# Token mixing moved behind the attention, and a new order for the first head: an attention and MLP-mixer kernel on one core

## Chip, core and metric

One core of a Trainium2 chip. The metric is the device time of one execution in microseconds (us), the lower the better; it is given as the median of repeated runs.

## What is computed

```python
# attention: B=2, H=8, S=768, D=64, 16 centroids for each head
q_assign = argmax(q_n @ c_n.T)          # q, k, centroids normalized; k_assign alike
scores = where(q_assign[:, None] == k_assign[None, :], q @ k.T / 8, -1e9)
x = softmax(scores) @ v                 # then heads side by side: x is [2, 768, 512]
# first mixer
xt = x.transpose(0, 2, 1)
u = x + (relu(xt @ w_tok1) @ w_tok2).transpose(0, 2, 1)    # token mixing, 256 wide
x = u + relu(u @ w_ch1) @ w_ch2                            # channel mixing, 1536 wide
# second mixer
theta = x @ w_theta
u = x + w_tok_r @ (x * cos(theta)) + w_tok_i @ (x * sin(theta))
out = u + relu(u @ w_ch)
```

The weights come as 64-bit floats; the kernel converts them on the chip.

## The kernel before

**Numbers.** A float32 operand is split into a rounded high part and the rest (names that end in `h` and `l`), and a product is three matmuls: low by high, high by low, high by high (`mm3`). `split_sb` and `split_ps` make such a pair. `load_w` fetches a 512 KB block of 64-bit weights by the SP queue into one of three buffers (`wraw`), and converts it: two copies on ACT (L100, L101), a shift and a combination on DVE (L103, L104), an addition on POOL (L107), and then a split. The addition is the last reader of the raw buffer.

**Attention.** There are 48 units: 2 batches, 8 heads, 3 pairs of 128-row query tiles (`b, h, u`; the index `n` of the loop runs over them). Tile names carry batch, head, query tile: `nm175` belongs to batch 1, head 7, tile 5. For each unit `scores` makes 8 matmuls of 384 columns and for each of two query tiles a row maximum on DVE (`nm`, L359) and an exponential on ACT (`e`, L361); `turn`, one unit later, transposes `e` in three pieces of four transposes (L376) and splits each into `ph` and `pl`, either by ACT and DVE (kind "A") or by ACT and POOL (kind "C": a copy `pr`, then `ph` and `pl`, L386 and L387); `values`, two units later, makes 12 matmuls of 256 columns (L399), copied and added into `xt` (`tmp` on ACT, L404; `xt` on DVE, L406). `masks` finds the centroid of each query and key of a pair of heads (`sim`, four DVE steps, `pp`, `oh`); the result goes as extra rows 64 to 79 into the operands `q2` and `k2`. `natural` transposes a finished pair of heads into the residual `xn`.

**First pair.** `load_pair` loads heads 0 and 1 together (`ql00`, `kl00`: 128 rows). For the operands `qh`, `q2`, `k1`, `k2` of heads 0 and 1, `prep_first` loads each of them again, twice each, to have a head's 64 rows on both halves of the partitions. All of `masks(0, 0)`, the placing of the centroids and the second head's operands stand ahead of the first unit. Matmuls on a constant tile (`warm_up`, 17, 4, 20 and 18 of them) run on TensorE at the start.

**Token mixing.** The six blocks of w_tok1 and w_tok2 are loaded and converted in units 2, 6, 10, 14, 18 and 22 (`W_AT`), each behind the mask rows' transfers. `tokens(b, half)` mixes 256 of the 512 columns of one batch: 36 matmuls `g` and 36 `h` of 256 columns, so 288 in all four calls. From unit 18 on one step of it (a split, a `g` of 18 matmuls, an `h` of 6) is written behind each unit; calls that are left follow the last unit.

**Behind it.** `u_turn` transposes `xn` (48 transposes, `u`), and from there the channel mixing starts (`r`), followed by the second mixer.

**Order.** The order on each engine is fixed at build time by a list scheduler, so code is a priority rather than a place; `issue_after` holds code back behind an instruction. Each engine runs its own rows in order, so what waits holds up all that stands behind it on that engine.

Of the kernel before, what the change touches and what calls it, by code (L numbers as in the profile page):

```python
# [18 lines left out]
P = 128  # L19
# [26 lines left out]
WARM = (17, 4, 20, 18)  # L46
# [3 lines left out]
def tile_model(ctx: ExitStack, tc: tile.TileContext, qT, kT, v, cent, w1, w2, wc1, wc2, wth, wri, wch, out):  # L50
# [40 lines left out]
    def load_w(src, name, pool=None):  # L91
# [18 lines left out]
        split_sb(h, l, w, "pa"[wcount[0] % 2], "p")  # L110
# [12 lines left out]
    with ExitStack() as actx:  # L123
# [45 lines left out]
        for j in range(2):  # L169
            r, n = slice(64 * j, 64 * j + 64), slice(96 + CL * j, 96 + CL * j + CL)  # L170
            nc.vector.tensor_copy(out=cst[r, n], in_=cps[r, CL * j : CL * j + CL])
# [33 lines left out]
        for t in q2 + k2:  # L205
            nc.gpsimd.memset(t[64:128, :].bitcast(F32), 0.0)

        def masks(b, pr):
# [28 lines left out]
            turned = nc.vector.transpose(out=eqT, in_=eq)  # L237
            marks.setdefault("eqT", turned)
# [4 lines left out]
            nc.tensor.matmul(pp, ltri, eqT, start=True, stop=True)  # L243
            nc.vector.scalar_tensor_tensor(out=oh, in0=pp, scalar=0.0, in1=eqT, op0=ALU.is_equal, op1=ALU.mult)
            if first:
                for a in range(2):
                    n = slice(a * NH, a * NH + NH)
                    r = 32 * a
                    nc.vector.tensor_copy(out=q2[0][64 : 64 + CL, n], in_=oh[r : r + CL, :])
                    r = 64 + 32 * a  # L250
                    if a == 0:
                        nc.scalar.activation(  # L252
                            out=k2[0][64 : 64 + CL, n], in_=oh[r : r + CL, :], func=AF.Copy, scale=BIG, bias=-BIG
                        )
                    else:
                        nc.vector.tensor_scalar(
                            out=k2[0][64 : 64 + CL, n], in0=oh[r : r + CL, :], scalar1=BIG, scalar2=-BIG,
                            op0=ALU.mult, op1=ALU.add,
                        )
# [7 lines left out]
        def prep_first(b, h):  # L267
# [15 lines left out]
            return qh, q2[i], k1, k2[i], load_v(b, h)  # L283

# [59 lines left out]
        def scores(b, h, u, ops):  # L344
# [3 lines left out]
            for j in range(2):  # L348
# [3 lines left out]
                for half in range(2):  # L352
                    n = slice(half * NH, half * NH + NH)
                    nc.tensor.matmul(ps[:, half, :NH], qh[:, c], k1[:, n], start=True, stop=False)  # L354
                    last = nc.tensor.matmul(ps[:, half, :NH], ql[:, c], kk[:, n], start=False, stop=True)  # L355
                    if (b, h, u) == (0, 0, 0):
                        marks["scores"] = last
                nm = ap.tile([P, 1], F32, tag="nm", bufs=4, name=f"nm{b}{h}{qt}")
                nc.vector.tensor_reduce(out=nm, in_=ps[:, :, :NH], axis=AX.XY, op=ALU.max, negate=True)  # L359
                e = ap.tile([P, S], F32, tag="e", bufs=4, name=f"e{b}{h}{qt}")  # L360
                nc.scalar.activation(  # L361
# [6 lines left out]
        def turn(b, h, u, es):  # L368

            pr = []  # L370
            for j in range(NT // 2):
                ps = ps_t.tile([P, 2, 256], F32, tag="t", name=f"t{b}{h}{u}{j}")
                for i in range(2):
                    for a in range(2):
                        kt = 2 * j + a
                        nc.tensor.transpose(ps[:, a, i * P : i * P + P], es[i][:, kt * P : kt * P + P], ident)  # L376
# [33 lines left out]
        def tokens(b, half):  # L410

            cols = slice(half * 256, half * 256 + 256)
            xs, gs = [], []

            def split_x(s):
                h, l = (fp.tile([P, 256], F32R, tag="fx", bufs=12, name=f"x{k}{b}{half}{s}") for k in "hl")
                split_sb(h, l, xn[b * NT + s][:, cols], XS[0], XS[1])
                xs.append((h, l))

            def up(t):  # L420
                ps = ps_t.tile([P, 512], F32, tag="t", name=f"g{b}{half}{t}")[:, :256]
                lw = []
                for s in range(NT):
                    o = (s % 2) * 256 + t * P
                    lw.append(tuple(w[:, o : o + P] for w in w1s[s // 2]))
                mm3(ps, list(zip(lw, xs)), True, True)
                h, l = (fp.tile([P, 256], F32R, tag="fg", bufs=4, name=f"g{k}{b}{half}{t}") for k in "hl")
                nc.scalar.activation(out=h, in_=ps, func=AF.Relu)
                nc.vector.scalar_tensor_tensor(
                    out=l, in0=ps, scalar=0.0, in1=h.bitcast(F32), op0=ALU.max, op1=ALU.subtract  # L430
                )
                gs.append((h, l))

            def down(s):
                ps = ps_t.tile([P, 512], F32, tag="t", name=f"h{b}{half}{s}")[:, :256]
                lw = []
                for t in range(NTT):
                    o = t * 256 + (s % 2) * P
                    lw.append(tuple(w[:, o : o + P] for w in w2s[s // 2]))
                mm3(ps, list(zip(lw, gs)), True, True)  # L440
                x = xn[b * NT + s][:, cols]
                nc.vector.tensor_tensor(out=x, in0=ps, in1=x, op=ALU.add)

            for s in range(NT):
                split_x(s)
                yield
            for t in range(NTT):
                up(t)
                yield
            yield  # L450
            for s in range(NT):
# [325 lines left out]
```

## Time and profile before

| | us |
|---|---|
| median of 3 runs (lowest to highest) | 691.19 (689.98 to 693.18) |
| profiled execution, its own time | 691.88 |
| its span | 690.2 |
| TensorE, matmuls busy | 659.0 |
| VectorE (DVE) busy | 436.5 |
| ScalarE (ACT) busy | 372.8 |
| GpSimd (POOL) busy | 387.2 |
| first row maximum starts | 17.26 |
| first matmul of the channel mixing starts | 312.32 |

Times in the trace count from the start of the span; 1.7 us of the execution's time lie outside it. A matmul's busy time includes its way through the array, so matmuls overlap and "busy" is more than the pace.

### The profile page before, as it was taken

To read this page: it belongs to the slowest core of one execution; us is meant where nothing else is said; L and a number is where in the kernel's file an instruction comes from. 1 tells how busy PE (TensorE), PEld (TensorE's weight loads), DVE (VectorE), ACT (ScalarE), POOL (GpSimd) and SP (SyncE) were. 2 spreads that over 40 slices of the span, in tenths; PEclk is the share of its full clock that TensorE was granted. 3 is DMA by queue.
4 is the path that set the end of the run, shared out by engine and by line. 5 is a ranking of instruction groups with operands and counts; after the bars stand their busy time and mean duration, and the time that the engine had idled before them with its cause. 6 is when DMAs were issued, how large, how long until landed. Compare 5 with 4: busy or idle time off the path is not lost.

```text
span 690.2 us, 10585 instructions
## 1 busy us (share of the span) xinstructions
PE 659.0 (95%) x3772; PEld 578.1 (84%) x3772; DVE 436.5 (63%) x710; ACT 372.8 (54%) x722; POOL 387.2 (56%) x376
## 2 busy tenths in 40 slices
PE   7899989889999999999999999999999999999998
PEld 4798878788998999897888888888888777888886
DVE  6788788978888968558664533445657876523122
ACT  3687768676968777526553431135668684320000
POOL 8977779685866664437884640331456797432000
PEclk9899989999999999999999999999999999999999
DMA  9545645476344330003442321030021233320001
GB/s 264 142 108 165 173 106 146 104 222 180 81 93 92 86 76 1 1 1 123 134 142 92 122 91 33 9 114 2 0 62 61 88 95 93 123 61 32 16 30 47
DMA packets 24533, 62.27 MB, mean 90 GB/s; under 512 B 4320, under 2 KB 7584, under 8 KB 24480
## 3 DMA queue, kind: packets, MB, share of 16 engines
q1 hardware_dynamic: 24480, 61.59, 32.1%
q8 instruction: 30, 0.49, 0.3%
q14 instruction: 23, 0.19, 0.1%
HBM read 40.44 MB, written 3.15 MB: 63 GB/s over the span
## 4 chain that ended last, share of the span: by engine, by line
PE 74%; DVE 6%; DMA 6%; ACT 5%; POOL 4%; issue 3%; SPq 2%; ACTq 0%; POOLq 0%; DVEq 0%
PE o L399 7%; PE t L376 6%; PE r L118 5%; PE r L119 5%; PE r L120 5%; PE c L118 5%; PE c L119 5%; PE c L120 5%; PE y L120 4%; PE y L118 4%; PE y L119 4%; PE s L354 3%; PE s L355 3%; DMA w_raw<-w 3%; ACT e L361 2%
## 5 line engine op out<-in xcount | busy, mean ns | idle before, releaser
L359 DVE TENSOR_REDUCE nm<-s 128x1 f32<-128x768 f32 x96 | 90.9, 949 | 20.9 <-PE s L355 20.3
L361 ACT ACTIVATE e<-s,nm 128x768 f32<-128x768 f32 x96 | 86.9, 906 | 23.0 <-DVE nm L359 12.7
L376 PE MATMUL t<-ident,e 128*128 128x128 f32 x576 | 80.6, 275 | 5.9 <-DVE pl L86 4.7
L399 PE MATMUL o<-ph,vs 128*128 128x256 f32 x288 | 77.3, 298 | 3.0 <-DVE xt L406 3.0
L354 PE MATMUL s<-k,qh 128*128 128x384 f32 x192 | 70.7, 369 | 9.0 <-ACT e L361 6.8
L376 PEld LDWEIGHTS t<-ident,e 128*128 128x128 f32 x576 | 67.8, 142 | 10.5 <-DVE pl L86 4.3
L399 PE MATMUL o<-pl,vs 128*128 128x256 f32 x288 | 74.8, 291 | 0.3 <-POOL pl L387 0.3
L86 DVE TENSOR_TENSOR pl<-t,ph 128x512 fp32r<-128x512 f32 x96 | 62.9, 678 | 6.5 <-ACT ph L85 4.8
L355 PE MATMUL s<-k,q 128*128 128x384 f32 x192 | 65.7, 343 | 1.3 <-ACT k L252 1.3
L85 ACT ACTIVATE ph<-t 128x512 fp32r<-128x512 f32 x96 | 54.9, 598 | 17.6 <-PE t L376 14.8
L387 POOL TENSOR_TENSOR pl<-pr,ph 128x512 fp32r<-128x512 f32 x48 | 62.9, 1310 | 2.0
L386 POOL TENSOR_SCALAR ph<-pr 128x512 fp32r<-128x512 f32 x48 | 30.3, 632 | 57.6 <-ACT pr L382 51.4
L399 PEld LDWEIGHTS o<-ph,vs 128*128 128x128 f32 x288 | 56.1, 195 | 4.0 <-DVE xt L406 3.7
L118 PE MATMUL r<-ul,c_h 128*128 128x512 f32 x144 | 56.7, 394 | 0.0
L399 PEld LDWEIGHTS o<-pl,vs 128*128 128x128 f32 x288 | 56.1, 195 | 0.5 <-POOL pl L387 0.5
L118 PE MATMUL y<-zl,k_h 128*128 128x512 f32 x144 | 56.1, 390 | 0.0
L120 PE MATMUL y<-zh,k_h 128*128 128x512 f32 x144 | 56.1, 389 | 0.0
L119 PE MATMUL y<-zh,k_l 128*128 128x512 f32 x144 | 56.0, 389 | 0.0
L119 PE MATMUL r<-uh,c_l 128*128 128x512 f32 x144 | 56.0, 389 | 0.0
L120 PE MATMUL r<-uh,c_h 128*128 128x512 f32 x144 | 55.9, 389 | 0.0
L120 PE MATMUL c<-c_h,rh 128*128 128x512 f32 x144 | 55.9, 389 | 0.0
L119 PE MATMUL c<-c_h,rl 128*128 128x512 f32 x144 | 55.8, 389 | 0.0
(201 smaller groups left out, 1686.3 us busy)
## 6 DMA issues: line engine op xcount, KB each, us to landing
c_raw<-wc SPq DMA_DIRECT2D x24, 512.0 KB, 3.4
k_raw<-wri SPq DMA_DIRECT2D x18, 512.0 KB, 3.6
qh<-qh SPq DMA_DIRECT2D x28, 192.0 KB, 3.0
k<-kh SPq DMA_DIRECT2D x28, 192.0 KB, 3.7
ql<-qT SPq DMA_DIRECT2D x8, 384.0 KB, 4.2
kl<-kT SPq DMA_DIRECT2D x8, 384.0 KB, 4.4
vr<-v SPq DMA_DIRECT2D x16, 192.0 KB, 3.3
w_raw<-w SPq DMA_DIRECT2D x6, 512.0 KB, 4.0
```

What stands on the lines that cost most here:

```text
L85: nc.scalar.activation(out=h, in_=ps, func=AF.Copy)
L86: nc.vector.tensor_tensor(out=l, in0=ps, in1=h.bitcast(F32), op=ALU.subtract)
L118: nc.tensor.matmul(ps, ah, bl, start=first and i == 0, stop=False)
L119: nc.tensor.matmul(ps, al, bh, start=False, stop=False)
L120: nc.tensor.matmul(ps, ah, bh, start=False, stop=last and i == n - 1)
L354: nc.tensor.matmul(ps[:, half, :NH], qh[:, c], k1[:, n], start=True, stop=False)
L355: last = nc.tensor.matmul(ps[:, half, :NH], ql[:, c], kk[:, n], start=False, stop=True)
L359: nc.vector.tensor_reduce(out=nm, in_=ps[:, :, :NH], axis=AX.XY, op=ALU.max, negate=True)
L361: nc.scalar.activation(out=e.rearrange("p (a n) -> p a n", a=2), in_=ps[:, :, :NH], func=AF.Exp, bias=nm, accum_out=sums[b, h // 2][:, qt, ...
L376: nc.tensor.transpose(ps[:, a, i * P : i * P + P], es[i][:, kt * P : kt * P + P], ident)
L387: nc.gpsimd.tensor_tensor(out=pl, in0=raw, in1=ph.bitcast(F32), op=ALU.subtract)
L399: nc.tensor.matmul(ps[:, :256], vs[:, kt, :], p[:, kt % 2, :], start=n == 0 and k == 0, stop=n == NT - 1 and k == 1,)
```

## The change

- **Token mixing** leaves the loop. `tok_x` splits batch 0's six blocks of `xn` on POOL in units 43 to 48; the weights are loaded (by priority) in units 46 and 47, with both halves of the split on ACT and DVE (`"av"`); then follow, for all 512 columns at once, `tok_x` of batch 1 (ACT and DVE), `tok_up` and `tok_down`: 144 matmuls of 512 columns in place of 288 of 256.
- **First head**: `prep_pair_first` makes head 0's operands out of `ql00` and `kl00`, with copies that shift partitions; head 0's four loads are gone, and the low part of `k1` is made by DVE, not POOL.
- **Behind the first maxima** go the mask row of head 1 (`m00`), head 1's operands, and `place_centroids`. Two of head 0's four mask-row copies go to ACT from DVE (one from DVE stays, ACT has three).
- The first two units split all pieces by kind "A". Clearing `q2` and `k2` of head 1 stands later on POOL. The last warm-up has 9 matmuls, not 18.

```diff
-FILL_AT = 18
-W_AT = {W0 + i * WD: (i,) for i in range(6)}
+X_AT = 43
+W_AT = {46: (0,), 47: (1, 2, 3, 4, 5)}
-WARM = (17, 4, 20, 18)
+WARM = (17, 4, 20, 9)
...
+        def prep_pair_first(ts):
+            q, k = (t[0:64, :] for t in ts)
...
+            marks["k1"] = nc.gpsimd.tensor_scalar(out=k1[0:64, :], in0=k, **one)
+            nc.scalar.activation(out=qh[0:64, :], in_=q, func=AF.Copy, scale=scale)
+            nc.vector.tensor_tensor(out=k1[64:128, :], in0=k, in1=k1[0:64, :].bitcast(F32), op=ALU.subtract)
+            nc.scalar.activation(out=qh[64:128, :], in_=q, func=AF.Copy, scale=scale)
...
-                kind = KINDS[3 * u + j]
+                kind = "A" if (b, h) == (0, 0) and u < 2 else KINDS[3 * u + j]
...
+                    with tc.issue_after(marks["max"].ins):
+                        next(first, None)
+                        ops[heads[1]] = prep_first(*heads[1])
+                    place(1, ms[0, 0])
+                    with tc.issue_after(marks["k1"].ins), tc.issue_after(marks["max"].ins):
+                        place_centroids()
...
-            if n >= FILL_AT and fills and next(fills[0], fills) is fills:
-                fills.pop(0)
-            if n in W_AT:
-                with tc.issue_after(placed[0].ins):
+            if 0 <= n - X_AT < NT:
+                tok_x(0, n - X_AT)
+            for i in W_AT.get(n, ()):
+                with tc.issue_after(marks["exp"].ins):
...
+        for s in range(NT):
+            tok_x(1, s)
+        tok_up(0, 0)
+        tok_up(0, 1)
+        tok_up(1, 0)
+        for s in range(NT):
+            if s == NT - 2:
+                tok_up(1, 1)
+            tok_down(0, s)
+        for s in range(NT):
+            tok_down(1, s)
```

**Order on DVE at the first maxima.** The rows up to the third maximum, before. `eqT` and `oh` are steps of the mask, `q2_1` and the mask rows `m00` are head 1's.

```order
L237 STREAM_TRANSPOSE eqT00_178<-eq00_176 128x384
L279 SCALAR_TENSOR_TENSOR q2_1_156<-qr01_208,qh01_214 64x768
L244 SCALAR_TENSOR_TENSOR oh00_180<-pp00_181,eqT00_178 128x384
L249 CAST q2_0_155<-oh00_180 16x384 x2
L256 TENSOR_SCALAR k2_0_157<-oh00_180 16x384
L262 TENSOR_SCALAR m00_188<-oh00_180,mab_150 128x384
L359 TENSOR_REDUCE nm000_245<-s000_240 128x1
L359 TENSOR_REDUCE nm001_254<-s001_249 128x1
L359 TENSOR_REDUCE nm002_318<-s002_313 128x1
```

The same place in the changed kernel:

```order
L239 STREAM_TRANSPOSE eqT00_189<-eq00_187 128x384
L245 SCALAR_TENSOR_TENSOR oh00_191<-pp00_192,eqT00_189 128x384
L253 CAST q2_0_155<-oh00_191 16x384
L374 TENSOR_REDUCE nm000_208<-s000_203 128x1
L374 TENSOR_REDUCE nm001_217<-s001_212 128x1
L257 TENSOR_SCALAR m00_221<-oh00_191,mab_150 128x384
L274 SCALAR_TENSOR_TENSOR q2_1_156<-qr01_223,qh01_229 64x768
L84 TENSOR_TENSOR ctl_141<-cps_135,cth_140 128x128
L177 CAST csth_138<-cth_140 64x4x16 x2
L374 TENSOR_REDUCE nm002_304<-s002_299 128x1
```

Head 1's `q2_1`, the mask row `m00` and the centroids' placing (`ctl`, `csth`) now stand between the second and the third maximum; one copy into `k2_0` and one into `q2_0` have left DVE.

**Order on ACT at a weight block.** Before, block w1_1 in unit 6, among the exponentials of head 2:

```order
L361 ACTIVATE e022_782,sm02_668<-s022_775,nm022_780 128x768
L100 ACTIVATE w1_1_f_765<-w1_1_raw_763 128x512
L101 ACTIVATE w1_1_raw_763<-w1_1_raw_763 128x512
L85 ACTIVATE ph0200_815<-t0200_810 128x512
L85 ACTIVATE ph0201_824<-t0201_819 128x512
L361 ACTIVATE e023_791,sm02_668<-s023_784,nm023_789 128x768
L404 ACTIVATE tmp012_852<-o012_839 64x256
```

In the changed kernel the first such rows (w1_0) stand directly ahead of the last unit's exponentials, and these behind them:

```order
L78 ACTIVATE w1_0_h_3840<-w1_0_f_3834 128x512
L83 ACTIVATE ph1720_3976<-t1720_3971 128x512
L83 ACTIVATE ph1721_3985<-t1721_3980 128x512
L397 ACTIVATE pr1722_3996<-t1722_3989 128x512
L99 ACTIVATE w2_0_raw_3935<-w2_0_raw_3935 128x512
L98 ACTIVATE w1_2_f_3925<-w1_2_raw_3923 128x512
L78 ACTIVATE w1_1_h_3919<-w1_1_f_3913 128x512
L419 ACTIVATE tmp171_4013<-o171_4000 64x256
L99 ACTIVATE w2_1_raw_3947<-w2_1_raw_3947 128x512
L98 ACTIVATE w2_0_f_3937<-w2_0_raw_3935 128x512
L78 ACTIVATE w1_2_h_3931<-w1_2_f_3925 128x512
L419 ACTIVATE tmp172_4033<-o172_4020 64x256
```

The copies of all six weight blocks now stand in one stretch around the last unit, with its copies `ph1720` to `tmp172` among them. The raw block of w2_1 takes the buffer that w1_1's leaves, so its transfer starts behind POOL's addition for w1_1.

**Order on TensorE at the end of the attention.** Before, matmuls of batch 0's second half (`h013`) among those of the last two units:

```order
L399 MATMUL o162_4102<-ph1622_4025,vs16_3585 128x256
L399 MATMUL o162_4102<-pl1622_4026,vs16_3585 128x256
L118 MATMUL h013_4118<-gl010_3653,w2_1_h_1753 128x256
L119 MATMUL h013_4118<-gh010_3652,w2_1_l_1754 128x256
L120 MATMUL h013_4118<-gh010_3652,w2_1_h_1753 128x256
L118 MATMUL h013_4118<-gl011_3739,w2_1_h_1753 128x256
L119 MATMUL h013_4118<-gh011_3738,w2_1_l_1754 128x256
L120 MATMUL h013_4118<-gh011_3738,w2_1_h_1753 128x256
L376 MATMUL t1710_4144<-ident_58,e172_4062 128x128 x2
```

In the changed kernel the last of `values`, the last transposes of `natural`, and then the first token matmuls:

```order
L414 MATMUL o172_4020<-ph1722_3994,vs17_3498 128x256
L414 MATMUL o172_4020<-pl1722_3995,vs17_3498 128x256
L468 MATMUL x130_4039<-ident_58,xt16_3465 128x128 x2
L468 MATMUL x134_4048<-ident_58,xt16_3465 128x128 x2
L116 MATMUL g00_4077<-xl00_3611,w1_0_h_3840 128x512
L117 MATMUL g00_4077<-xh00_3610,w1_0_l_3841 128x512
L118 MATMUL g00_4077<-xh00_3610,w1_0_h_3840 128x512
L116 MATMUL g00_4077<-xl01_3695,w1_0_h_3840 128x512
L117 MATMUL g00_4077<-xh01_3694,w1_0_l_3841 128x512
```

No matmul of the token mixing stands ahead of the transposes `x130` and `x134` any more, so the first of them waits, in order, for the last copy into `xt`.

## Rows read from the trace of the kernel before

**Rows 1.** Time windows, maxima alone (L359): us, DVE busy (count), clock, DMA.

```profile
31.70:50.85 19.15, 7.57 (x8) 1.00 0.54 122
50.85:185.10 134.25, 43.62 (x46) 0.96 0.56 146
185.10:273.50 88.40, 32.28 (x34) 1.00 0.35 77
273.50:312.30 38.80, 1.90 (x2) 1.00 0.01 1
```

**Rows 2.** The same windows, all work: PE, PEld, DVE, ACT, POOL busy (count), clock, DMA.

```profile
31.70:50.85 19.15, 18.73 (x143) 17.90 (x142) 17.23 (x28) 16.75 (x36) 13.96 (x15) 1.00 0.54 122
50.85:185.10 134.25, 119.92 (x850) 113.90 (x849) 112.51 (x186) 102.54 (x217) 102.14 (x105) 0.96 0.56 146
185.10:273.50 88.40, 87.38 (x661) 84.51 (x660) 72.89 (x130) 67.10 (x143) 54.32 (x60) 1.00 0.35 77
273.50:312.30 38.80, 36.57 (x300) 35.08 (x299) 22.12 (x48) 17.48 (x39) 15.60 (x18) 1.00 0.01 1
```

**Rows 3.** Windows, matmuls `g` alone, then `h` alone, and what handles them.

```profile
50.85:185.10 134.25, 4.69 (x36) 4.42 (x36) 0.84 (x2) 0.77 (x2) 0.96 0.56 146
185.10:273.50 88.40, 4.62 (x36) 4.44 (x36) 0.85 (x2) 0.76 (x2) 1.00 0.35 77
...
50.85:185.10 134.25, 1.75 (x12) 1.56 (x12) 0.83 (x2) 0.96 0.56 146
185.10:273.50 88.40, 6.38 (x42) 5.49 (x42) 2.90 (x7) 1.00 0.35 77
```

**Rows 4.** Chain of waits: start us, length us, what.

```profile
133.41 1.43 PE o L399 x12
139.33 5.32 DMA w_raw<-w
```

**Rows 5.** Timeline, then chain, at the channel mixing's start: start us, length us.

```profile
306.30 1.15 PE L561 MATMUL u<-ident,xn 128*128 128x128 f32 x9
...
312.32 0.47 PE r L118
312.79 0.23 PE r L119
```

**Rows 6.** Weight blocks by operation: count, ns least, median, most; then their transfers.

```profile
L103 DVE TENSOR_SCALAR w_raw<-w_f x6: 419/429/1994, 26.1 to 145.4; 128x512 uint32<-128x512 uint32 x6
L104 DVE SCALAR_TENSOR_TENSOR w_f<-w_f,w_raw x6: 683/1076/1681, 26.6 to 145.9; 128x512 uint32<-128x512 uint32 x6
L107 POOL TENSOR_TENSOR w_f<-w_f,w_raw x6: 1300/1302/1308, 28.0 to 147.3; 128x512 uint32<-128x512 uint32 x6
...
DMA to landing us min/median/max: 3.8/4.0/5.3
```

**Rows 7.** Costliest groups: shapes, count, busy us, mean ns, idle before.

```profile
L361 ACT ACTIVATE e<-s,nm 128x768 f32<-128x768 f32 x96 | 86.9, 906 | 23.0 <-DVE nm L359 12.7 <-PE t L376 9.2 <-ACT xh L80 0.3
L86 DVE TENSOR_TENSOR pl<-t,ph 128x512 fp32r<-128x512 f32 x96 | 62.9, 678 | 6.5 <-ACT ph L85 4.8 <-PE o L399 0.9
L406 DVE TENSOR_TENSOR xt<-o,tmp 64x256 f32<-64x256 f32 x48 | 19.8, 412 | 6.0 <-ACT tmp L404 5.1
```

**Rows 8.** Windows around a fall of the clock; columns as in Rows 2.

```profile
75.00:90.00 15.00, 11.30 (x74) 10.04 (x73) 11.61 (x18) 11.29 (x23) 12.91 (x12) 0.98 0.65 160
90.00:105.00 15.00, 14.37 (x90) 14.15 (x90) 12.52 (x25) 9.94 (x22) 11.03 (x12) 0.79 0.51 120
```

**Rows 9.** Timeline of the start: start us, length us, engine, line, tile.

```profile
10.99 2.08 POOL L282 TENSOR_TENSOR k<-kr,k 64x768 fp32r<-64x768 f32 x1
14.55 1.30 DVE L249 CAST q<-oh 16x384 fp32r<-16x384 f32 x2
17.26 1.80 DVE L359 TENSOR_REDUCE nm<-s 128x1 f32<-128x768 f32 x2
17.30 4.06 PE L140 MATMUL wps<-warm 128*128 128x256 bf16 x18
```

More of the change, by code (lines that the diff above doesn't have):

```diff
@@ L1 @@
 import math
-from contextlib import ExitStack
+from contextlib import ExitStack, nullcontext
 import concourse.bass as bass
@@ L236, in masks @@
             eqT = mp.tile([P, NH], BF16, tag="eq", bufs=2, name=f"eqT{b}{pr}")
[L237 to L238 removed]
+            nc.vector.transpose(out=eqT, in_=eq)
             yield
@@ L242, in masks @@
             pp = ps_t.tile([P, 512], F32, tag="t", name=f"pp{b}{pr}")[:, :NH]
-            nc.tensor.matmul(pp, ltri, eqT, start=True, stop=True)
+            marks["cl"] = nc.tensor.matmul(pp, ltri, eqT, start=True, stop=True)
             nc.vector.scalar_tensor_tensor(out=oh, in0=pp, scalar=0.0, in1=eqT, op0=ALU.is_equal, op1=ALU.mult)
@@ L408, in values @@
             )
[L410 to L442, printed above, removed]
-            for s in range(NT):
-                split_x(s)
-                yield
-            for t in range(NTT):
[L448 to L451, printed above, removed]
-                down(s)
-                yield
@@ L455, in natural, with tok_down @@
+        def tok_down(b, s):
+            ps = ps_t.tile([P, 512], F32, tag="t", name=f"h{b}{s}")
+            lw = []
+            for t in range(NTT):
+                o = t * 256 + (s % 2) * P
+                lw.append(tuple(w[:, o : o + P] for w in w2s[s // 2]))
+            mm3(ps, list(zip(lw, gs[b])), True, True)
+            x = xn[b * NT + s]
+            nc.vector.tensor_tensor(out=x, in0=ps, in1=x, op=ALU.add)
         def natural(b, pr):
@@ L475, in tile_model @@
         raws = load_pair(0, 0)
-        for _ in masks(0, 0):
-            pass
-        ops = {heads[0]: prep_first(*heads[0])}
-        with tc.issue_after(marks["eqT"].ins):
-            ops[heads[1]] = prep_first(*heads[1])
-        place(1, ms[0, 0])
-        place_centroids()
+        first = masks(0, 0)
+        next(first)
+        vs00 = load_v(0, 0)
+        with tc.issue_after(marks["cst"].ins):
+            ops = {heads[0]: prep_pair_first(raws) + (vs00,)}
+        for _ in range(4):
+            next(first)
+        with tc.issue_after(marks["k1"].ins):
+            clear(1)
         gen = iter(())
-        w1s, w2s = [], []
+        w1s, w2s, xs, gs = [], [], {}, {}
         units = [(b, h, u) for b, h in heads for u in range(NT // 2)]
         es, prs = {}, {}
-        fills, late = [], []
+        late = []
         for n in range(len(units) + SKEW):
@@ L511, in tile_model @@
                         gen = masks(*pr)
-            for _ in range(PACE):
-                next(gen, None)
             if n == 42:
@@ L517, in tile_model @@
                 prs[n - 1] = turn(*units[n - 1], es.pop(n - 1))
+            with tc.issue_after((marks["turn"] if n else marks["scores"]).ins) if n < 3 else nullcontext():
+                for _ in range(PACE):
+                    next(gen, None)
             if 0 <= n - SKEW:
```

93 lines of the change are left out of this document (55 added, 38 removed).

## The prediction

> **What bounds the kernel now.** I read the busy times by engine first (TensorE 659.0 of 690.2 us), then windows that count the row maxima, then the same windows for all engines and for the token mixing's matmuls, and last the chain of waits.
>
> There are two maxima for each unit. Between 31.7 and 273.5 us stand 8 + 46 + 34 = 88 of the 96, so 44 units: three units' six maxima come before, and the last unit's two behind [rows 1]. These 241.8 us are 5.50 us per unit. They hold 126 of the token mixing's 288 matmuls (36 + 36 `g`, 12 + 42 `h`, [rows 3]); at 1.43 us for 12 matmuls of 256 columns [rows 4], 0.12 each, that is 15.1 us. So 226.7 us are attention, 5.15 us per unit. Stretch by stretch, without that fill:
>
> - 31.7 to 50.85: 4 units in 19.15 us, 4.79 each, TensorE busy 18.7 [rows 1, 2].
> - 50.85 to 185.1: 23 units in 134.25 - 48 x 0.12 = 128.5, 5.59 each. TensorE is busy 119.9 of 134.25, at a mean clock of 0.96 [rows 2].
> - 185.1 to 273.5: 17 units in 88.4 - 78 x 0.12 = 79.0, 4.65 each, TensorE busy 87.4 of 88.4 at full clock [rows 2].
>
> The reader is to see that the attention can run near 4.7 with fill (third stretch) and without (first), and that the middle one is loose. Five of the six weight blocks are converted in it (the last from 145.9, [rows 6]), and the chain passes through a block's transfer, 5.32 us from 139.33 [rows 4]: ACT reached the copy before its data had landed, and the exponentials behind it stood still. When TensorE was busy 11.3 of 15 us its granted clock fell to a mean of 0.79 in the next 15 us, a mix of its two levels (1.2 and 2.4 GHz) that takes 0.21 x 15 = 3.2 us of work [rows 8].
>
> From the last unit's first maximum (273.5) to the first `r` (312.3) pass 38.8 us, with the other 162 token matmuls in them, 19.4 us. From `r` on the kernel is the same; those 377.9 us I leave as they are.
>
> **The change, part by part.**
>
> *Start: -3.0 us (bounds -1 and -4.5).* TensorE's first scores waited for POOL's subtraction of 2.08 us that began at 10.99 [rows 9]. DVE now makes that low part, from rows that are there earlier. Of the four copies into `q2` and `k2`, DVE did two in 1.30 us and then a third; now DVE does one and ACT three, side by side. I take 2.2 us off the first maximum (17.26, [rows 9]). Behind the second maximum four pieces of work (`m00`, `q2_1`, `ctl`, `csth`) come ahead of the third, some 3 us as an estimate from the first maximum's neighbours; they lie where DVE had waited for 18 warm-up matmuls of 4.06 us [rows 9]. With 9 of them TensorE is free 2.0 us earlier, but DVE then sets the pace, so the third maximum keeps about the same gain. The first weight block's shift and combination (0.43 + 1.08, [rows 6]) leave units 0 and 1, two splits of 0.68 [rows 7] come to DVE there for two on a late POOL: 0.8 us more. The low bound is the copies on ACT being as slow as they were on DVE; the high one, the whole 2.08 and 2.0.
>
> *Attention, 44 units: -30.6 us.* 15.1 of it is fill that goes elsewhere; the rest is pace. I take 4.8 us per unit, next to the first stretch, which has neither fill nor a block's transfer in the way, and a little over the third: 44 x 4.8 = 211.2 in place of 241.8. Bounds: 4.65 (TensorE full) gives 204.6; 5.15 (the mean now) 226.7. What is left in the units is covered: POOL's split of batch 0's six blocks (at most 2 x 1.3 each, by the 1.30 of a POOL addition of that size, [rows 6]) falls in the last five units, where POOL is busy 54.3 of 88.4 us [rows 2]; 15.6 us of work against about 9 us of gaps by that share, but two blocks need no buffer of the attention's and can go earlier. If POOL is late, the `pl` of kind "C" is late next. The three w1 transfers at the start go behind head 1's loads on SP's queue; ahead of them nothing waits, and behind them stand the pair 1 loads, which POOL needs only after head 1's work.
>
> *End: +20.2 us, 59 in place of 38.8 (bounds 54 and 66).* From the last unit's first maximum:
>
> 1. First token matmul at 18.5. It stands behind `x130` and `x134`, so behind the last `xt`. Up to that copy DVE has 2 maxima (1.80, [rows 9]), 4 low parts of pieces and 3 of weights (7 x 0.68), 4 `xt` (4 x 0.41, [rows 7]), 4 shifts (0.43) and 4 combinations (1.08, [rows 6]), 4 small `xn` and a reciprocal (2.5 as an estimate): 16.7 us. On top comes a wait. POOL adds w1_1 at some 7.5, 1.30 long, after DVE's combination; only then can w2_1 be fetched, which lands 4.0 us later [rows 6], near 13. ACT's copy of it is in order ahead of w2_0's copy, w1_2's high part and `tmp172`; DVE's shift for w2_0 waits for that, with `xt` behind it: 2 us. Bounds: 14 (no wait, records overlapping) and 25.
> 2. 144 matmuls of 512 columns at 0.23 [rows 5]: 33.1 us.
> 3. Batch 1's splits on ACT stand behind copies of channel blocks c1_0 to c1_2, each of which waits for a buffer and 4.0 us of transfer; by the same count the fourth `xh` is some 1 us late. Bounds 0 and 4.
> 4. From the first `u` to the first `r` 312.3 - 306.3 = 6.0 us as before [rows 5], and 0.4 for the last addition.
>
> In the first 18.5 us TensorE has only about 9 us of its own. That idle time is what the fill covered before, and it is priced in the 18.5.
>
> *Widths.* Rows: 288 x 0.12 = 34.6 us [rows 4] become 33.1 [rows 5], so the wider matmuls save 1.5, which is in the sums above. The Trainium skill ("TensorE: Matmul & The Clock Gate", "Back-to-back issue gap") gives an isolated matmul its columns over 2.4 GHz and 2.5 ns more: an estimate of 31.4 us before and 31.1 after, a saving of 0.4. The trace is slower by a tenth for both widths; by the page the total would be 1 us higher.
>
> *Sum.* -3.0 - 30.6 + 20.2 = -13.4. The profiled execution took 691.9 us, 0.7 over the median: 678.5 in its terms, 678 as a median. With p us per unit the sum is 44p - 224.6: nothing is gained at p = 5.10.
>
> **Rivals.** 0.5% (3.5 us) is about what a measurement of this kernel can tell from no change.
>
> *The holes stay (slower).* The token matmuls filled holes that the waits between ACT, DVE and TensorE leave; taken out, the units last as long as with them. For it: the middle stretch had no fill up to `g` and was the loosest. Against it: its blocks' transfers are gone, and the first stretch had no fill either. At p = 5.3 the time is 691.9 + 8.6 = 700.5, 0.7 less as a median; it is slower by 0.5% from p = 5.19. The Trainium skill ("Perfetto Trace Analysis", "Optimization Strategy") speaks against this change: where stages have different busiest engines, it advises to interleave them. By that rule the 44 units keep their 241.8 us, and the time would be 709. The third stretch agrees with the rule (TensorE busy 99% with fill), the first one does not need it.
>
> *The weights hold no pace.* Something else, such as the copies for the next head on SP's queue, made the middle stretch slow: p 5.0 to 5.15, 687 to 694.
>
> *The end starves.* The six blocks, the last unit and batch 1's splits share ACT and DVE in one stretch; the first token matmul comes at 25 rather than 18.5, and the clock falls after the idle time as in [rows 8]: 678 + 6.5 + 3.2 = 688.
>
> *All of it fits.* p = 4.65 and an end of 54: -3.0 - 37.2 + 15.2 = -25, 666 as a median.
>
> **The numbers.** My forecast (p 4.7 to 4.95, an end of 56 to 63; 671 to 686) 0.64; holes stay 0.06; no pace from the weights 0.07; the end starves 0.12; all fits 0.11. The predicted time is 678. The range is 666 to 689: the forecast, most of "all fits" and half of "the end starves". Faster by over 0.5% is the forecast, "all fits" and a quarter of "the end starves" and of "no pace": 0.80. Within 0.5%: 0.13. Slower: 0.07.
>
> **What would show it.** First maximum near 15 us. No weight transfer in the chain between 30 and 230 us, and no fall of the clock there; 44 units in 205 to 218 us; if over 224, the pace was wrong. From the last unit's first maximum 16 to 22 us to the first `g`, with ACT waiting for w2_1's transfer; then `g` and `h` at 0.23, first `r` near 299. Wrong would be a channel mixing that starts without its first block, or that runs slower than its 377.9 us because its blocks are fetched later.

## The result and the profile after

The changed kernel takes 695.35 us (median of 7 runs, 694.29 to 698.18) beside 691.0 for the kernel before: a ratio of 1.0071, interval 1.0054 to 1.0089. It is slower by 0.7%; the forecast was 678, faster. The profiled execution has a span of 693.6 us in place of 690.2.

Cut at the marks that the prediction used (first maximum of unit 3, first maximum of the last unit, first `r`), the span divides so:

| | before | forecast | after |
|---|---|---|---|
| start, to unit 3 | 31.79 | 28.8 | 34.43 |
| 44 units | 241.8 | 211.2 | 215.6 |
| end, to the first `r` | 38.7 | 59 | 64.0 |
| from the first `r` | 377.9 | 377.9 | 379.5 |

Every term is over its forecast: by 5.6, 4.4, 5.0 and 1.6 us, 16.6 in all.

The stretches of the changed kernel, all engines (start, units, the wait for the first token matmul, token mixing, transposes for channel mixing), to be read beside [rows 2]:

```profile
core 0: us, PE busy (x) PEld busy (x) DVE busy (x) ACT busy (x) POOL busy (x), PEclk, DMA share, GB/s
14.70:34.40 19.70, 14.59 (x80) 13.06 (x79) 15.68 (x20) 10.25 (x20) 9.44 (x8) 0.83 0.47 139
34.40:250.10 215.70, 207.91 (x1533) 198.19 (x1531) 185.31 (x319) 169.60 (x353) 148.39 (x154) 1.00 0.47 108
250.10:268.40 18.30, 10.80 (x69) 9.20 (x68) 16.45 (x29) 14.43 (x29) 12.13 (x10) 0.91 0.31 89
268.40:306.10 37.70, 34.33 (x146) 26.77 (x147) 23.09 (x34) 12.29 (x21) 7.07 (x5) 1.00 0.21 69
306.10:314.10 8.00, 5.91 (x50) 5.18 (x48) 6.96 (x11) 6.42 (x12) 5.92 (x5) 1.00 0.14 40
```

The maxima alone in the first two stretches, beside [rows 1]:

```profile
core 0: us, DVE busy (x), PEclk, DMA share, GB/s
14.70:34.40 19.70, 5.65 (x6) 0.83 0.47 139
34.40:250.10 215.70, 83.00 (x89) 1.00 0.47 108
```

Six maxima and then 89, the last of which is the last unit's first: 44 units in 215.6 us, 4.90 each. TensorE is busy 207.9 of 215.7 us at full clock; the loose middle stretch of [rows 2] is gone, and with it the fall of the clock in [rows 8]. What the reader is to see in the other rows is TensorE's share: 14.6 of 19.7 us at a mean clock of 0.83 at the start, 10.8 of 18.3 in the wait for the first token matmul.

The start on DVE, from the first maximum on (in place of the last rows of [rows 9]):

```profile
14.77 1.82 DVE L374 TENSOR_REDUCE nm<-s 128x1 f32<-128x768 f32 x2 [0.95 <-PE s L372]
16.51 1.11 DVE L257 TENSOR_SCALAR m<-oh,mab 128x384 fp32r<-128x384 f32 x1
17.54 1.57 DVE L274 SCALAR_TENSOR_TENSOR q<-qr,qh 64x768 fp32r<-64x768 f32 x1
19.03 0.27 DVE L84 TENSOR_TENSOR ctl<-cps,cth 128x128 fp32r<-128x128 f32 x1
19.23 2.40 DVE L177 CAST csth<-cth 64x64 fp32r<-64x64 f32 x2
21.66 0.96 DVE L374 TENSOR_REDUCE nm<-s 128x1 f32<-128x768 f32 x1
22.65 1.07 DVE L177 CAST cstl<-ctl 64x64 fp32r<-64x64 f32 x2
```

Between the second maximum and the third stand 5.4 us of work (1.11, 1.57, 0.27 and 2.40). The two casts of `csth` take 2.40 us; in the kernel before they took 0.49, at 6.73 us, when POOL was about to fall idle, and in cent_ahead (below) 0.67. Here a POOL subtraction of 2.51 us runs beside them from 18.27. The Trainium skill ("GPSIMD Engine Reference", "Key points") says that GpSimd and VectorE share SBUF interfaces and get in each other's way for some forms of VectorE's instructions; these rows fit that if the casts are of such a form, but no run here takes POOL's work away to show it.

What TensorE does meanwhile, in windows of 2 us (columns as in the first view):

```profile
22.00:24.00 2.00, 0.30 (x2) 0.30 (x3) 1.92 (x4) 1.34 (x3) 1.47 (x1) 1.00 0.51 171
24.00:26.00 2.00, 1.35 (x5) 0.87 (x4) 1.97 (x4) 1.13 (x3) 0.83 (x1) 0.56 0.68 194
26.00:28.00 2.00, 2.00 (x8) 2.00 (x8) 1.49 (x3) 0.41 (x1) 0.00 (x0) 0.50 0.04 11
28.00:30.00 2.00, 2.00 (x11) 2.00 (x10) 0.00 (x0) 0.58 (x2) 0.00 (x0) 0.50 0.00 0
30.00:32.00 2.00, 2.00 (x11) 1.90 (x11) 0.74 (x1) 0.53 (x1) 0.00 (x0) 0.74 0.00 0
```

TensorE has 0.30 us of work from 22 to 24 us, and in the windows behind that the granted clock is 0.56, 0.50, 0.50 and 0.74: the lower level, 1.2 GHz, for about 6.8 us by these shares. From 25.6 us on it works without a break, on the second and third units above all.

A stretch at the lower level is not new at the start. The kernel before has one as long, from 14 to 22 us:

```profile
14.00:18.00 4.00, 2.82 (x10) 2.16 (x11) 3.89 (x6) 1.80 (x2) 3.92 (x5) 0.55 0.84 324
18.00:22.00 4.00, 4.00 (x21) 3.14 (x20) 1.06 (x2) 1.88 (x4) 3.92 (x5) 0.60 0.28 54
```

There it lies on the first scores and on the 18 warm-up matmuls, which is why these last 4.06 us in [rows 9]; here it lies on the units themselves.

The end: first TensorE's rows that had waited (time waited and releaser in the brackets), then DVE's rows around the two longest waits.

```profile
258.16 0.38 PE L414 MATMUL o<-ph,vs 128*128 128x256 f32 x1 [2.24 <-DVE xt L421]
...
263.61 0.58 PE L414 MATMUL o<-ph,vs 128*128 128x256 f32 x1 [2.86 <-DVE xt L421]
...
268.27 0.44 PE L468 MATMUL x<-ident,xt 128*128 128x128 f32 x2 [1.43 <-DVE xt L421]
...
279.12 0.50 PE L116 MATMUL g<-xl,w_h 128*128 128x512 f32 x1 [0.65 <-DVE xl L80]
...
282.48 0.50 PE L116 MATMUL g<-xl,w_h 128*128 128x512 f32 x1 [1.69 <-DVE xl L80]
```

```profile
255.38 0.60 DVE L101 TENSOR_SCALAR w_raw<-w_f 128x512 uint32<-128x512 uint32 x1
256.01 1.64 DVE L102 SCALAR_TENSOR_TENSOR w_f<-w_f,w_raw 128x512 uint32<-128x512 uint32 x1
257.69 0.42 DVE L421 TENSOR_TENSOR xt<-o,tmp 64x256 f32<-64x256 f32 x1
258.14 1.52 DVE L80 TENSOR_TENSOR w_l<-w_f,w_h 128x512 fp32r<-128x512 f32 x1
259.58 1.27 DVE L84 TENSOR_TENSOR pl<-t,ph 128x512 fp32r<-128x512 f32 x2
260.85 0.93 DVE L101 TENSOR_SCALAR w_raw<-w_f 128x512 uint32<-128x512 uint32 x1
261.82 0.69 DVE L102 SCALAR_TENSOR_TENSOR w_f<-w_f,w_raw 128x512 uint32<-128x512 uint32 x1
262.43 0.68 DVE L80 TENSOR_TENSOR w_l<-w_f,w_h 128x512 fp32r<-128x512 f32 x1
263.14 0.42 DVE L421 TENSOR_TENSOR xt<-o,tmp 64x256 f32<-64x256 f32 x1
```

`xt` of 257.69 and of 263.14 release TensorE. Ahead of each stand steps of the weight blocks (`w_raw`, `w_f`, `w_l`), 2.2 us ahead of the first and 2.3 ahead of the second. At 279 and 282 TensorE waits for batch 1's remainders `xl`. The last stretch, from the last `h` to the first `r`, beside [rows 5]:

```profile
306.14 4.53 PE L580 MATMUL u<-ident,xn 128*128 128x128 f32 x40
311.13 0.66 PE L580 MATMUL u<-ident,xn 128*128 128x128 f32 x4 [0.47 <-DVE ul L84]
312.79 0.66 PE L580 MATMUL u<-ident,xn 128*128 128x128 f32 x4 [1.00 <-DVE ul L84]
314.08 0.52 PE L116 MATMUL r<-ul,c_h 128*128 128x512 f32 x1 [0.63 <-DVE ul L84]
```

Three waits, 2.10 us in all, for `ul`, which DVE makes between steps of channel mixing's blocks: 7.9 us for what took 6.0. Behind it the clock is at the lower level again from 314.4 to 317.8 us, which is the 1.6 us of the table's last row.

### The profile page after: what moved, and what is told of

Its sections match the earlier page's. It is cut to its first block, busy times and chain, and to the rows that moved or that the text cites. A ratio compares the mean times of both kernels' runs of the same rounds, so it can differ in the third digit from the quotient of the medians.

```text
span 693.6 us, 10136 instructions
## 1 busy us (share of the span) xinstructions
PE 658.5 (95%) x3619; PEld 569.0 (82%) x3619; DVE 447.6 (65%) x707; ACT 373.5 (54%) x706; POOL 367.4 (53%) x350
## 3 DMA queue, kind: packets, MB, share of 16 engines
q1 hardware_dynamic: 24160, 60.80, 31.4%
## 4 chain that ended last, share of the span: by engine, by line
PE 48%; POOL 4%; ACT 3%; issue 2%; DVE 2%; DMA 2%; DVEq 0%; POOLq 0%; ACTq 0%
PE r L116 5%; PE r L117 5%; PE r L118 5%; PE c L116 4%; PE c L117 4%; PE c L118 4%; PE y L118 4%; PE y L117 4%; PE y L116 4%; PE po L116 2%; PE po L118 2%; PE po L117 2%; DMA ch_raw<-wch 1%; PE h L116 1%; POOL r L631 1%
## 5 line engine op out<-in xcount | busy, mean ns | idle before, releaser
L374 DVE TENSOR_REDUCE nm<-s 128x1 f32<-128x768 f32 x96 | 90.5, 948 | 16.7 <-PE s L372 16.0
L371 PE MATMUL s<-k,qh 128*128 128x384 f32 x188 | 68.9, 369 | 7.8 <-ACT e L376 7.4
L84 DVE TENSOR_TENSOR pl<-t,ph 128x512 fp32r<-128x512 f32 x98 | 64.3, 678 | 8.5 <-ACT ph L83 7.9
L414 PEld LDWEIGHTS o<-ph,vs 128*128 128x128 f32 x288 | 55.9, 194 | 10.5 <-DVE xt L421 8.6
L402 POOL TENSOR_TENSOR pl<-pr,ph 128x512 fp32r<-128x512 f32 x46 | 59.4, 1292 | 2.2
L118 PE MATMUL c<-c_h,rh 128*128 128x512 f32 x144 | 55.9, 389 | 0.0
```

Of the source, the lines that this page charges most:

```text
L84: nc.vector.tensor_tensor(out=l, in0=ps, in1=h.bitcast(F32), op=ALU.subtract)
L118: nc.tensor.matmul(ps, ah, bh, start=False, stop=last and i == n - 1)
L374: marks["max"] = nc.vector.tensor_reduce(out=nm, in_=ps[:, :, :NH], axis=AX.XY, op=ALU.max, negate=True)
L402: nc.gpsimd.tensor_tensor(out=pl, in0=raw, in1=ph.bitcast(F32), op=ALU.subtract)
L414: nc.tensor.matmul(ps[:, :256], vs[:, kt, :], p[:, kt % 2, :], start=n == 0 and k == 0, stop=n == NT - 1 and k == 1,)
```

## Experiments

Medians, ratios to the kernel before with their intervals, and the same three marks; the last column is the span from the first `r` on. The kernels ran in several batches, each beside the kernel before, whose median lay between 689.8 and 691.9 us; kernels of different batches are compared by their ratios.

| run | us | ratio (interval) | unit 3 | 44 units | end | rest |
|---|---|---|---|---|---|---|
| mix_only | 688.8 | 0.9961 (0.9944 to 0.9978) | 29.76 | 212.5 | 65.3 | 379.0 |
| start_only | 694.0 | 1.0034 (1.0007 to 1.0060) | 32.14 | 244.5 | 37.7 | 377.7 |
| start_act | 692.6 | 1.0028 (1.0010 to 1.0047) | 29.29 | 246.6 | 37.7 | 379.6 |
| mask_step | 689.0 | 0.9988 (0.9972 to 1.0004) | 31.59 | 239.4 | 38.7 | 377.5 |
| warm18 | 694.4 | 1.0040 (1.0023 to 1.0057) | 34.34 | 214.8 | 64.1 | 379.2 |
| cent_ahead | 692.2 | 1.0016 (0.9998 to 1.0034) | 31.66 | 215.6 | 66.0 | 378.4 |
| cent_act | 689.9 | 0.9973 (0.9956 to 0.9989) | 27.95 | 216.2 | 65.9 | 378.0 |
| after_gen | 690.3 | 0.9998 (0.9983 to 1.0012) | 34.83 | 210.8 | 64.9 | 379.3 |
| gen_back | 685.0 | 0.9912 (0.9887 to 0.9938) | 27.92 | 211.7 | 63.5 | 377.8 |
| early_w | 702.0 | 1.0130 (1.0094 to 1.0167) | 35.33 | 228.5 | 55.2 | 379.6 |
| early_w2 | 705.5 | 1.0195 (1.0153 to 1.0237) | 34.26 | 231.4 | 55.9 | 377.7 |
| mix_early | 695.6 | 1.0071 (1.0044 to 1.0097) | 30.68 | 228.4 | 55.9 | 377.7 |
| up_only | 685.3 | 0.9914 (0.9888 to 0.9939) | 28.50 | 216.0 | 59.9 | 379.9 |
| best_up | 680.2 | 0.9847 (0.9821 to 0.9872) | 27.86 | 210.9 | 61.3 | 377.8 |
| hold_c | 686.4 | 0.9941 (0.9918 to 0.9963) | 28.93 | 211.1 | 58.2 | 388.4 |
| hold_c_x1 | 687.1 | 0.9953 (0.9933 to 0.9974) | 28.79 | 211.3 | 59.5 | 387.5 |

**The halves.** The start's hunks alone in the kernel before, and the token mixing's hunks alone. The mask steps' new place behind the transposes went with the start.

> The kernel before with the new start alone (first head's operands from its pair's rows, second head, mask rows and centroids' placing behind the first maxima, nine warm-ups in place of eighteen); token mixing and its weights stay between the units. Theory (the new start loses what it was forecast to win: the first maximum comes 2.5 us earlier, but the first maximum of unit 3, at 31.79 before, comes at about 34.4 as in the changed kernel, and nothing later takes the 2.65 us back): 693 to 695, first maximum of unit 3 at 34 to 35. Rival one (the start wins its forecast 3.0 us as long as token mixing stays where it was): 687 to 689. Rival two (what is late at unit 3 is taken back by unit 10, since the units are held by something else): 690 to 692.

> The changed kernel with the start of before (copies of the first two heads, masks and centroids ahead of the first unit, eighteen warm-ups); token mixing follows the attention as in the changed kernel. Theory (start costs 2.65 us, the move of token mixing by itself takes from the attention about what it adds behind it, and a little more): 692 to 693.5, 44 units in 214 to 217 us. Rival (the start has no part in the loss): 695 to 696. Rival two (the start wins 3 us): 697 to 699.

Token mixing alone makes the kernel faster by 0.4%, more than expected. In the profiled executions 2.0 us of this stand ahead of unit 3 (29.76 in place of 31.79), where TensorE is at the lower clock for 3.4 us in place of 6.8. The start alone makes the kernel slower, by as much as the theory says, but not by its way: unit 3 comes 0.4 us late and not 2.7, and another 2.7 us are lost in the 44 units. Together they cost 4.4 us where the sum of the two is -0.6: something costs only when both are there.

**The start.** Three ways to relieve it in the changed kernel.

```diff
-WARM = (17, 4, 20, 9)
+WARM = (17, 4, 20, 18)
```

> The changed kernel with eighteen warm-up matmuls behind the first scores, as before, in place of nine. Theory one (the half-clock stretch of TensorE at 24.2 to 31.1 us, which lies on the second unit's matmuls, comes from TensorE's idle time behind the nine, and more warm-ups keep the full clock): 692 to 694, no granted clock below 0.9 in 24 to 34 us. Theory two (VectorE's work between the second and the third maximum is what is late, 1.11 + 1.57 + 0.27 + 4.80 us, and the clock only follows): 695 to 697, first maximum of unit 3 at 34 to 36.

The clock still falls (0.50 from 24 to 28 us), and unit 3 comes at 34.34; the time, 694.4, lies between the two ranges. The missing warm-ups are not the cause. At the full clock the 18 take 2.14 us here, in place of the 4.06 of [rows 9].

```diff
             ops = {heads[0]: prep_pair_first(raws) + (vs00,)}
+            place_centroids()
...
-                    with tc.issue_after(marks["k1"].ins), tc.issue_after(marks["max"].ins):
-                        place_centroids()
```

> The changed kernel with the centroids' placing (the split and four small casts) ahead of the first head's one-hots, as before; the rest of the new start stays. Theory (VectorE's pile behind the second maximum, 6.4 us long in the changed kernel, 2.67 of it the centroids, lets TensorE idle until its clock halves at 24.2 us): third maximum at 18.5 to 20 in place of 21.66, no half clock in 24 to 31, first maximum of unit 3 at 30 to 32.5 in place of 34.43, total 690.5 to 693. Rival one (the mask rows and the second head's remainder, 2.7 us, are enough for the fall): unit 3 at 33 or later, 694 to 696. Rival two (ahead of the first maxima the casts delay those by as much as they give back): first maximum at 16.5 or later, 694 to 696.

Half right: unit 3 is 2.8 us earlier, but the first maximum is 1.2 later and the clock still falls (0.60 and 0.54 from 24 to 28 us). The remainder `q2_1` now takes 2.59 us in place of 1.57.

```diff
-                    nc.vector.tensor_copy(out=dst[r, :, n], in_=...)
+                    nc.scalar.activation(out=dst[r, :, n], in_=..., func=AF.Copy)
```

> The changed kernel with the four casts of the centroids' placing on ScalarE in place of VectorE, behind the first maxima as in the change. Theory (VectorE's pile): third maximum at 19 to 20 in place of 21.66, first maximum of unit 3 at 30 to 33 in place of 34.43, total 690.5 to 693.5. Rival (VectorE's pile is cover only, TensorE waits for the exponentials or its clock falls anyhow): unit 3 at 34 or later, 694.5 to 696.

DVE's rows there, in place of the seven above:

```profile
15.70 0.82 DVE L258 TENSOR_SCALAR m<-oh,mab 128x384 fp32r<-128x384 f32 x1
16.44 1.76 DVE L275 SCALAR_TENSOR_TENSOR q<-qr,qh 64x768 fp32r<-64x768 f32 x1
18.13 0.28 DVE L84 TENSOR_TENSOR ctl<-cps,cth 128x128 fp32r<-128x128 f32 x1
18.33 1.80 DVE L375 TENSOR_REDUCE nm<-s 128x1 f32<-128x768 f32 x2
```

Third and fourth maximum follow at once, the clock stays at its full level, and unit 3 comes at 27.95, 6.5 us earlier; on ACT two of the casts take 0.52. Of the 6.5 us, 0.8 stand ahead of the first maximum (13.96 in place of 14.77), which lies anywhere from 13.96 to 14.90 in the kernels with this same start. The total is 5.5 us under the changed kernel's. VectorE's pile was the cause of the late unit 3.

start_act puts the same four casts on ScalarE in start_only:

> The kernel before with the new start alone, as start_only, and with the centroids' four small casts on ScalarE. Theory (without those casts in VectorE's way the start wins what was forecast, and the win stays): first maximum of unit 3 at 28 to 29 in place of 31.79, 688 to 690. Rival (unit 3 is as early, but units that wait for the weights' transfers give it back by unit 13): 690.5 to 693.

The rival holds: unit 3 is 2.9 us earlier than in start_only, and the time is the same (1.0028 beside 1.0034). The 2.5 us won on the kernel before at unit 3 are gone behind units 12 and 13 (16.0 us for the two, 10.8 before), where ACT stands still for a weight block:

```profile
79.94 0.66 ACT L101 ACTIVATE w_f<-w_raw 128x512 f32<-128x512 f32 x1 [3.72 <-DMA w_raw<-w]
```

That is one of several such places: at unit 13 start_act is 3.5 us behind the kernel before, at unit 16 it is 1.1 ahead, at the last unit 2.3 behind. Which of them decides, the rows do not show.

**The mask steps.** after_gen is the changed kernel, gen_back is cent_act, each with the steps back in front; mask_step is the opposite move in the kernel before.

```diff
+            if n >= 3:
+                for _ in range(PACE):
+                    next(gen, None)
...
             prs[n - 1] = turn(*units[n - 1], es.pop(n - 1))
-            with tc.issue_after(...) if n < 3 else nullcontext():
+            if n < 3:
+              with tc.issue_after(...):
```

> cent_act with the masks' two steps per unit given out ahead of the unit's transposes again, as in the kernel before, for all units from the fourth on; the change had put them behind the transposes. Theory (the 3 to 4 us by which the 44 units of after and cent_act last longer than those of mix_only, 215.6 and 216.2 against 212.5, come from this place in the order): 44 units in 212 to 214, 686 to 688. Rival (they come from the start's other edits, or only from where the last unit's maximum falls): 44 units in 215.5 to 217, 689 to 691.

> The changed kernel with only the mask steps ahead of the transposes again from the fourth unit on. Theory (the attention's miss, 215.6 against the forecast 211.2, is this place in the order): 44 units in 211 to 213 us, first maximum of unit 3 still at 34 to 35, 690 to 692. Rival (it is the start's late order that the units keep, and gen_back was fast only with the start mended): 44 units in 214.5 or more, 694 to 696.

> The kernel before with one line moved: from the fourth unit on, the two mask steps of each unit are given out behind the unit's transposes, as the change has them, and no longer ahead of them. Theory (this place in the order costs the units time wherever token mixing is): 44 units in 244 to 248 us in place of 241.8, 693 to 696. Rival (with fill between the units it does not matter; what start_only and start_act lost between units 3 and 13 came from the start): 690 to 692.

The 44 units of after_gen, all engines:

```profile
34.80:245.60 210.80, 204.69 (x1512) 194.94 (x1511) 183.57 (x315) 167.26 (x349) 147.82 (x154) 1.00 0.48 110
```

210.8 us, and TensorE waits 6.1 of them in place of 7.8. The place of the steps costs 4.8 us of the units in the changed kernel and 4.5 with the start mended, and the ratios of the whole kernels move with it (1.0071 to 0.9998, 0.9973 to 0.9912). In the kernel before it costs nothing, against my theory: it counts only where token mixing has left the units. So it is with the casts, which cost 1% in the changed kernel and next to nothing in start_only. These two are what start_only and mix_only did not show apart.

Of the 4.8 us, 1.7 are waits. About half of the 4.8 is work that changes sides of a mark: between the marks the trace of the changed kernel has 528 matmuls of `values` and 530 transposes of `turn`, that of after_gen 516 and 522. These 20 matmuls, 2.4 us at 0.12 each, after_gen does behind the last unit's first maximum, where TensorE has time for them: its first token matmul comes 19.8 us behind that mark in place of 18.4. Nor is it an even price per unit, for 3.6 us of the difference stand at unit 12. That the place costs is shown; through which order, I did not settle.

**The weights.** Each block's transfer is issued long before its conversion, so that nothing waits for its landing, and both halves of its split go to POOL. The edit of early_w2 and mix_early, cut:

```diff
-W_AT = {46: (0,), 47: (1, 2, 3, 4, 5)}
+W_AT = {28: 0, 31: 1, 34: 2, 37: 3, 40: 4, 43: 5}
...
```

> The changed kernel with the six weight blocks of token mixing turned to float32 one by one during units 26 to 41 (rounding and remainder on POOL), each transfer issued long before, so that no engine waits for it; token mixing itself stays behind the attention. Theory (attention is now held by TensorE, whose idle time is 7.8 of 215.7 us, so that the blocks lie beside it at no cost; behind the attention the waits for the weights and for batch 1's remainders on VectorE go, some 3 to 5 us): 690 to 693, with 44 units in 214 to 218 us. Rival (ScalarE and VectorE hold the units' pace as soon as they carry a block, some 1 us for each): 44 units in 220 or more, 695 to 698. A rival by which the weights never mattered behind the attention: 695 to 696 with the pace unchanged.

> As early_w, with the blocks held behind the exponentials of their units 28, 31, 34, 37, 40 and 43, as the changed kernel holds its own (in early_w the compiler's order let the first two blocks go before the first maxima, so that it did not test this). Theory (TensorE holds the attention's pace, the blocks lie beside it; behind the attention the waits for weights and remainders shrink): 44 units in 214 to 218 us, first token matmul 14 to 17 us after the last unit's first maximum in place of 18.4, 690 to 693. Rival (ScalarE and VectorE hold the pace): 44 units in 220 or more, 697 to 701.

> The changed kernel with the start of before, the six weight blocks early as in early_w2, and both first layers of batch 0's token mixing given out at the last two steps of the attention, before the last transposes and the last batch's splits. Theory (what mix_only showed, 688.8, and the blocks cost the units nothing; TensorE's idle time between the last unit's values and the first token matmul, some 6 us, is filled): 682 to 686. Rival (blocks in the attention cost its pace as much as they free behind it): 688 to 692.

In early_w nothing held the blocks, and the compiler's order put the steps of two of them ahead of the first maxima (18.34 us); early_w2 mends that. The theory that TensorE alone holds the units falls. Beside after and mix_only the units of early_w2 and mix_early take 16 us longer, and the end gives back 8 to 9. Some of the 16 are steps of channel mixing's first blocks, whose buffers come free earlier; from unit 27 to unit 39, with four blocks and none of those, mix_early falls 7.9 us behind mix_only, 2.0 a block. The stretch of early_w2 from 150 us on (all engines), and TensorE's longest waits in it (total, times, longest):

```profile
150.00:265.00 115.00, 100.50 (x719) 92.77 (x718) 98.70 (x166) 88.19 (x183) 91.94 (x93) 1.00 0.46 116
```

```profile
PE s L378 <- ACT e L383: 6.8, 9, 1.9
PE t L398 <- DVE pl L85: 2.4, 1, 2.4
PE o L421 <- DVE xt L428: 2.3, 3, 0.9
```

TensorE is busy 87% of it, DVE 86% and POOL 80%; it waits for exponentials, low parts and additions. The longest of these waits (2.36 us, at 246.72) is for a low part that stands on DVE behind two steps of a block, 0.78 and 1.57 us long.

**The end.** up_only is cent_act with these two edits (cut; the low parts of w_tok2's blocks go to POOL), best_up is gen_back with them:

```diff
+            if n in UP_AT:                     # {48: 0, 49: 1}
+                tok_up(0, UP_AT[n])
...
+            with tc.issue_after(marks["xt"].ins):
+                w2s.append(load_w(*src, wp, "ap", raw))
```

> cent_act with another end: batch 0's two first layers are given out at the last two steps of the attention, and w_tok2's three blocks are converted behind the last unit's additions, with their remainders on POOL in place of VectorE. The attention's units are as in cent_act. Theory (the end is long because the last unit's low parts and additions stand on VectorE among the weights' shifts, combinations and remainders, and TensorE has nothing else in hand): first token matmul 12 to 15 us after the last unit's first maximum in place of 18.6, 60 to 62.5 us to the first matmul of channel mixing in place of 65.9, 685 to 687. Rival (the first token matmul comes earlier, but batch 1's remainders hold the rest as before): 688.5 to 690.5.

> gen_back and up_only together. If both theories hold their gains add: 682 to 685. If only the end's: 685 to 687. If neither: 689 to 691.

up_only's time is as expected; its first token matmul comes 10.3 us behind the last unit's first maximum, earlier than expected. best_up lies under its range. The gains of the three mends add: 695.35, 689.9, 685.0, 680.2 (ratios 1.0071, 0.9973, 0.9912, 0.9847). best_up is faster than both kernels.

hold_c is best_up with channel mixing's second to fourth blocks held behind the last `ul`; hold_c_x1 moves batch 1's remainders to POOL besides.

> best_up, with the second to fourth blocks of channel mixing converted only behind the last split of the transposed rows (their transfers as before). Theory (between the last token matmul and the first of channel mixing VectorE and ScalarE do these blocks' steps among the splits that TensorE waits for, 7.95 us in place of 6.0 before): 6.0 to 6.6 us there, 677.5 to 679.5. Rival (the second block is then late for the first of its 36 matmuls, 8.3 us on): 680 to 682.

> hold_c, with the remainders of batch 1's rows on POOL in place of VectorE. Theory (TensorE's waits of 0.7, 0.5 and 0.7 us on these remainders, 2.3 us in the changed kernel, come from VectorE's load): 676 to 678. Rival (POOL makes them more slowly than TensorE takes them, and the waits grow): 678 to 681.

From the last `h` to the first `r` pass 5.5 us in place of 7.9, so DVE's mixture of steps was the cause. But 10.7 us are lost behind it, and both kernels are slower than either expectation. TensorE's first matmul of a later part of channel mixing, and ACT's rows ahead of it:

```profile
403.90 0.77 PE L124 MATMUL c<-c_l,rh 128*128 128x512 f32 x1 [4.07 <-ACT rh L656]
```

```profile
402.07 0.65 ACT L107 ACTIVATE th_raw<-th_raw 128x512 uint32<-128x512 uint32 x1 [4.00 <-DMA th_raw<-wth]
402.63 0.64 ACT L106 ACTIVATE th_f<-th_raw 128x512 f32<-128x512 f32 x1
403.18 1.07 ACT L656 ACTIVATE rh<-r 128x512 fp32r<-128x512 f32 x2
```

The blocks stay late in a row until ACT stands 4.00 us before the transfer of a block of w_theta with `rh` queued behind it, and TensorE waits 4.07. Behind it the granted clock is 0.50, 0.50 and 0.67 in the three windows of 2 us from 404 us on, another 2.7 us of work. With POOL TensorE waits once for a remainder, 1.30 us, in place of 0.70, 0.51 and 0.74, but the end is 1.3 us longer: nothing won.

## Why the prediction was wrong

*What bounds it* held in the main. The middle stretch was loose because of the weights: without them 44 units take 211 to 216 us. But I had put it down to the blocks' transfers, and with these out of the way four blocks still cost 2.0 us each by their steps (mix_early). The Trainium skill ("Perfetto Trace Analysis", "Optimization Strategy"), which I had weighed as a rival, says that interleaving stages with different busiest engines may help; here mix_only, which takes the interleaving out, is faster by 0.4%, most of it ahead of unit 3, so that from there on the two orders are about even.

*Start.* This step failed in sign: +2.6 us in place of -3.0. The first maximum came about as forecast (14.77 for 15.1). The step that failed is "some 3 us as an estimate ...; they lie where DVE had waited for 18 warm-up matmuls", and "the third maximum keeps about the same gain". The four pieces took 5.4 us, 2.4 of it the casts; in the trace before, among other neighbours, the same pieces take 0.87, 1.22, 0.29 and 0.49, the 3 us of the estimate. Nor was the wait for the warm-ups still there to cover them: its 4.06 us were 18 matmuls at the lower clock, and the nine of the change take 1.16:

```profile
14.75 1.16 PE L138 MATMUL wps<-warm 128*128 128x256 bf16 x9
```

So the third maximum came at 21.66, only 0.4 us before that of the kernel before, and behind it TensorE ran dry and then at half its clock, which cost another 3.1 us up to unit 3. With the casts off VectorE (cent_act) the term is -3.9.

*Attention.* 215.6 in place of 211.2, inside its bounds. The pace of 4.8 was about right; what I put at nothing, without a reason, is the mask steps' move behind the transposes. It is in the edit, but neither the list of the change nor its cut diff shows it. With it undone the units take 210.8, or about 4.85 each with the 20 matmuls that then lie behind the mark.

*End.* 64.0 in place of 59, inside its bounds. The first token matmul came at 18.4 (forecast 18.5), with VectorE busy for 16.5 us (forecast 16.7) and ACT waiting for w2_1's transfer (1.35 us, up to 263.10): this part was right by its mechanism too. The 144 matmuls and their waits took 37.7 in place of 34.1: batch 1's remainders cost 2.3 us in place of 1.0; waits of 0.78 for an addition into `xn` and 0.25 for the low part of `g` were not in the sum; and without all waits a matmul takes 0.238 us, not 0.23. The "6.0 us as before" from `u` to `r` became 7.9. Taken as a sum this term was too small by a wait at each of its seams; up_only shows that most of it can be had back.

*Widths.* "The trace is slower by a tenth for both widths" was misread: by the prediction's own figures it is a tenth for 256 columns (34.6 over 31.4 us) and 6% for 512 (33.1 over 31.1).

*Rest.* It was taken as unchanged; it grew by 1.6 us through the clock at its beginning. gen_back, best_up and cent_act, whose clock does not fall there, take 377.7 to 378.0.

*The rivals.* "The holes stay" and "the weights hold no pace" are out (p is 4.90, and 4.79 in after_gen). "The end starves" named the right stretch, but gave the first matmul at 25; it came at 18.4, and the loss lay behind it. None had a start that loses, and the range ended at 689 for want of it.

## What to carry to other kernels

Work that is moved "behind" the first result of a pipeline still has to fit between that result and the next: sum the moved instructions on their new engine with the durations that they have beside the new neighbours, and ask whether TensorE runs dry there. A fill that leaves a loop takes its cover along: an order of steps that cost nothing with the fill in (mask_step) cost about 5 us without it, so each line of a diff that moves has to be priced in the new loop. And test edits one by one: a gain of 5.9 us (gen_back) and two losses of about 5 each hid in one change; with the losses mended and the end reordered the same idea stands 10.6 us under the kernel before.

## Unexpected of the hardware

Two casts of 64x64 took 0.49 us on VectorE in one place, 0.67 in another (cent_ahead) and 2.40 beside a POOL subtraction; on ScalarE two take 0.52.

TensorE's granted clock was at its lower level for about 6.8 us near the start both before and after the change. Before, it lay on the first scores and on warm-up matmuls; after, behind a stretch in which TensorE had little work, it lay on the second and third units. What a fall costs depends on what it falls on. Nor is it the same from kernel to kernel with one start: from 14 to 16 us the granted clock is 1.00 in the changed kernel and 0.53 in after_gen, which has the same code up to unit 3.
